# Late units of a state-space attention kernel: carry and scores in 32x32 tiles, heads paired q with 7-q, and one token per partition from the fifth unit on

## The chip, the cores and the metric

The kernel runs on one core of a Trainium2 chip. A core has TensorE (PE in the profile, with its weight loads as PEld), VectorE (DVE), ScalarE (ACT), GpSimd (POOL) and SyncE (SP), which issues most DMAs. Each engine works through its own list of instructions in order. The metric is the device time of one execution in microseconds (us).

## The reference

Two stages follow each other. The first is a chunked state-space attention with 4 batches, 8 heads, 768 tokens, head width 32 and state width 16:

```python
for c in range(nc):                       # chunks of the sequence
    cum = np.cumsum(log_a[chunk])
    L = np.exp(cum[:, None] - cum[None, :]) * causal
    y_intra = ((C @ B.T) * L) @ x         # inside the chunk
    y_inter = (C @ state) * np.exp(cum)   # from the state before
    state = np.exp(sum(la)) * state + B.T @ (x * np.exp(cum[-1] - cum))
```

The second is a feed-forward stage over all 3072 tokens (256 wide): `h = max(x @ w_in, 0)`, then `(h * h) @ w_out`, with 2048 hidden columns.

## The kernel before, in words

The tokens are cut into 12 units of 256 (three blocks of each of four batches); unit k is batch k mod 4, block k div 4. A unit is worked in two halves of 128 tokens, i = 0 and 1. The decay is folded into C and x beforehand (products with cumulated decay and with its reciprocal), so that the scores need only a causal mask.

For each unit, in this order:

- C, B and x are loaded by SyncE (`ph_load`, lines 121 to 136). Units below `LATE` (6) are loaded with two neighbouring tokens per partition in one DMA; later ones with one token per partition, one DMA for each half (line 129), and the x of units 8, 10 and 11 in two groups of heads besides.
- GpSimd scales C (`prep_c`, line 167), copies B to bf16 (`prep_b`, line 175) and scales x (`prep_x`, line 187). C and B land in `jt`, four heads side by side, heads q and q + 4 in one group of 32 columns.
- From unit 4 on a transposing DMA (`dma_tr`, line 196) makes `bct` of `jt`; before that TensorE does it.
- A *region* (`region`, line 421; from unit 4 on one per unit, named `rg4` to `rg12`) then does on TensorE, for the unit before (y) and the new one (u): the carry of y (the state times C, `ph_carry`, 128x128 matmuls against a block-diagonal spread state), the state update of u (`ph_u`), the products of y's masked scores with x (`ph_intra`), and the scores of u (`ph_mt`, lines 229 and 235). ScalarE copies y's result to `T` (`ph_t`) and u's update to `us`. VectorE masks u's scores (`ph_mask`, line 244), one bank of PSUM after another.
- VectorE advances the state (`ph_z`), and GpSimd spreads it over a block-diagonal tile `Sd` (`ph_sd`, line 371), which the next carry reads as weights.

Between the regions TensorE does the feed-forward stage of earlier units: `mm1` (line 450, four matmuls of 256 columns), ReLU on ScalarE (line 459), the square on VectorE (line 465), and `mm2` (line 481). From `rg4` on, PSUM banks 0 to 3 are the scores', 7 is `mm2`'s, and 4 to 6 go round between `mm1` and the regions, which take two.

The order of the work is written out by hand in the string `ORDER` (lines 48 to 69): each engine gets its instructions in the order in which the tokens stand there. A token is, for example, `ld4` (load unit 4), `pb5` (B of unit 5), `sa3` (spread state of unit 3, first half), `ml` (the mask of late units), `c1` (`mm1` and ReLU) or `C1` (`mm2`). On GpSimd the part around the first region reads `px4 pb5 pc5 sa3 px5 pq afC2 pc6 sa4`, and on SyncE `ld4`, C and B of unit 5, the transposes of unit 4 (`tr4`), x of unit 5, C of unit 6, `tr5`.

Of the kernel before, what the change touches and what calls it, by code (L numbers as in the profile page):

```python
# [30 lines left out]
def kernel(  # L31
# [38 lines left out]
    LATE = 6  # L70
# [23 lines left out]
    quad = const.tile([128, 4], FP32, name="quad")  # L94
# [11 lines left out]
    Pquad = const.tile([128, 24, 4], FP32, name="Pquad")  # L106
# [54 lines left out]
    def prep_c(k, eng, P=None):  # L161
        b, j = UNITS[k]
        p = P_sb if P is None else P
        st = 96 if P is None else 32
        col = (j * 32 if P is None else 0) + b * 8
        for g in range(2):
            eng.tensor_tensor(  # L167
                out=_fap(jt[k % 3], 128 + 144 * g, [[384, 2], [32, 4], [1, 16]]),
                in0=_fap(loaded[k]["C"], 128 * g, [[16, 2], [32, 4], [1, 16]]),
                in1=_fap(p, col + 4 * g, [[st, 2], [1, 4], [0, 16]]), op=ALU.mult)  # L170

    def prep_b(k, eng, gs=None):
        fn = eng.copy if eng is nc.scalar else eng.tensor_copy
        if gs is None:
            fn(out=_fap(jt[k % 3], 0, [[384, 2], [16, 2], [32, 4], [1, 16]]),  # L175
               in_=_fap(loaded[k]["B"], 0, [[16, 2], [128, 2], [32, 4], [1, 16]]))
            return
# [46 lines left out]
    def ph_mt(k):  # L224
        v = live[k]
        bct = v["bct"]
        for i in range(2 if k >= LATE else 0):
            for q in range(4):
                nc.tensor.matmul(pp[:, q, i * 256:i * 256 + 256], bct[32 * q:32 * q + 32, i, 0, :],  # L229
                                 _fap(bct[32 * q:32 * q + 32], i * 384 + 128, [[1, 256]]),  # L230
                                 start=True, stop=True, skip_group_check=True, tile_position=(32 * q, 0))
        for r in range(0 if k >= LATE else 2):
            for u in range(2):
                for q in range(4):
                    nc.tensor.matmul(  # L235
                        pp[64 * u:64 * u + 64, q, r * 256:r * 256 + 256],
                        bct[32 * q:32 * q + 32, r, 0, u * 64:u * 64 + 64],
                        _fap(bct[32 * q:32 * q + 32], 128 + u * 64, [[128, 2], [384, 2], [1, 64]]),
                        start=True, stop=True, skip_group_check=True,
                        tile_position=(32 * q, 64 * u))  # L240
        v["mts"] = big.tile([128, 4, 2, 2, 128], BF16, tag="mts", name=f"mts{k}")
# [21 lines left out]
    def ph_carry(k, h, begun):  # L263
        for i in range(2):
            S_i = live[k]["S"][i]
            if S_i is None:
                continue
            for g in range(2):
                mm(begun, h[i], range(4), pp[:, h[i], g * 128:(g + 1) * 128], S_i[:, g * 128:(g + 1) * 128],
                   _fap(live[k]["bct"], i * 384 + 128 + g * 128, [[1, 128]]) if k >= LATE else  # L270
                   _fap(live[k]["bct"], 128 + g * 128 + i * 64, [[384, 2], [1, 64]]), None)

    def ph_u(k, h, begun):
# [3 lines left out]
        if k >= LATE:  # L277
            for i in range(2 - last):
                for q in range(4):
                    mm(begun, h[i], [q], pp[32 * q:32 * q + 32, h[i], 256:320], jt[k % 3][:, i, 0, 32 * q:32 * q + 32],  # L280
                       _fap(v["xs"], i * 256 + q * 32, [[128, 2], [1, 32]]), (0, 32 * q))
            return
        for r in range(2):
            for i in range(2 - last):
                for q in range(4):
                    mm(begun, h[i], [q], pp[32 * q:32 * q + 32, h[i], 256:320],
                       jt[k % 3][64 * i:64 * i + 64, r, 0, 32 * q:32 * q + 32],
                       _fap(v["xs"][64 * i:64 * i + 64], r * 256 + q * 32, [[128, 2], [1, 32]]),
                       (64 * i, 32 * q))

    def ph_intra(k, h, begun, qs=range(4)):
        v = live[k]
        if k >= LATE:
            for i in range(2):
                for g in range(2):
                    for q in qs:
                        hd = 4 * g + q
                        mm(begun, h[i], [q], pp[32 * q:32 * q + 32, h[i], g * 128:(g + 1) * 128],
                           v["xs"][:, i, hd * 32:hd * 32 + 32], _fap(v["mts"], q * 512 + i * 256 + g * 128, [[1, 128]]),
                           (0, 32 * q))  # L300
            return
        for g in range(2):
            for r in range(2):
                for i in range(2):
                    for q in qs:
                        hd = 4 * g + q
                        mm(begun, h[i], [q], pp[32 * q:32 * q + 32, h[i], g * 128:(g + 1) * 128],
                           v["xs"][64 * i:64 * i + 64, r, hd * 32:hd * 32 + 32],
                           v["mts"][64 * i:64 * i + 64, q, r, g, :], (64 * i, 32 * q))

    def ph_t(k, h, engs=None):
        T[k] = tpool.tile([128, 2, 2, 2, 64], BF16, tag="T", name=f"T{k}")
        if k >= LATE:
            if h[1] == h[0] + 1:
                nc.scalar.copy(out=_fap(T[k], 0, [[128, 2], [256, 2], [1, 128]]),
                               in_=_fap(pp, h[0] * 512, [[512, 2], [128, 2], [1, 128]]))
                return
            for i in range(2):
                nc.scalar.copy(out=_fap(T[k], i * 128, [[256, 2], [1, 128]]), in_=_fap(pp, h[i] * 512, [[128, 2], [1, 128]]))
# [44 lines left out]
    def ph_sd(k, i):  # L364
        b, j = UNITS[k]
        v = live[k]
        if j == 2 and i == 1:
# [5 lines left out]
            in1=_fap(Pquad, 4 * total(i, b, j), [[0, 2], [1, 4], [0, 32]]), op=ALU.mult)  # L373
# [5 lines left out]
    def ph_sd_first(k):  # L379
# [6 lines left out]
            in1=_fap(Pquad, 4 * total(0, b, 0), [[0, 2], [1, 4], [0, 32]]), op=ALU.mult)  # L386
# [34 lines left out]
    def region(y=None, u=None, mt=None, late=False):  # L421

        h = sorted((bank(), bank()))
        begun = set()
        if y is not None:
            ph_carry(y, h, begun)
# [4 lines left out]
        if mt is not None:  # L431
# [10 lines left out]
    def mm1(blk, fp, c=None, h=None):  # L442
# [5 lines left out]
        for i in range(2):  # L448
            for g in range(2):
                nc.tensor.matmul(pp[:, h, i * 256:(i + 1) * 256] if c is None else  # L450
                                 _fap(pp, h * 512 + i * 256 + c * 64, [[128, 2], [1, 64]]),
                                 _fap(w, g * w.shape[2] + (o // 2) * 512 + 2 * (o % 2) + i, [[4, 128]]),
                                 T[blk][:, g].rearrange("p r u t -> p (r u t)") if c is None else T[blk][:, g, :, c],
                                 start=(g == 0), stop=(g == 1), skip_group_check=True)
# [18 lines left out]
    def mm2(blk, fp, rs=(0, 1), cols=None):  # L473
        h2 = h2s[(blk, fp)]
        gi, o = group_of(WOUT, fp)
        for i in range(2):
            for r in rs:
                first = fp == 0 and i == 0 and (r == 0 or blk == NU - 1)
                for c0, c1 in ((0, 256),) if cols is None and (blk < NU - 1 or r == 0) else cols or ((0, 128), (128, 256)):
                    dst = acc(blk, r) if c1 - c0 == 256 else pp[:, 1 + c0 // 128, 0:128]  # L480
                    nc.tensor.matmul(dst, h2[:, i, r * 128:(r + 1) * 128],  # L481
                                     w_out_b[gi][:, 2 * o + i, c0:c1], start=first, stop=(fp == 7 and i == 1),
                                     skip_group_check=True)
# [37 lines left out]
    with tc.manual_schedule():  # L521
# [47 lines left out]
        def quads():  # L569
            keep_if(quad, ones_f[:, 0:4], [[-32, 4]], 0, 1)  # L570
            keep_if(quad, quad, [[32, 4]], 31, -1)
# [11 lines left out]
        def picked():  # L583
            A.copy(out=_fap(spread, 0, [[32, 4], [16, 2], [1, 16]]), in_=_fap(heads, 0, [[1, 4], [4, 2], [0, 16]]))
# [14 lines left out]
        def first_quad():  # L599
            V.tensor_tensor(out=Pquad[:, 0:8], in0=_fap(pp, 4 * 512 + 64, [[1, 8], [0, 4]]),  # L600
                            in1=_fap(quad, 0, [[0, 8], [1, 4]]), op=ALU.mult)
# [27 lines left out]
        def second_quad():  # L629
            P.tensor_tensor(out=Pquad[:, 8:24], in0=_fap(Ptot, 8, [[1, 16], [0, 4]]),  # L630
                            in1=_fap(quad, 0, [[0, 16], [1, 4]]), op=ALU.mult)
# [110 lines left out]
        ups = {}  # L742

# [7 lines left out]
        def one(t):  # L751
# [5 lines left out]
            if len(name) == 1 and name.lower() in "abcdefghijkl" and len(f[0]) == 2:  # L757
# [7 lines left out]
                return  # L765
            if name[0] in "xryw" and len(name) == 2 and name[1] in "abcd":
                blk = "abcd".index(name[1])
                if name[0] in "xy":
                    ups[blk, k] = mm1(blk, k, None if name[0] == "x" else 0)
                    busy.add(ups[blk, k])  # L770
                elif name[0] == "w":
                    mm1(blk, k, 1, ups[blk, k])
                else:
                    busy.discard(ups[blk, k])
                    relu(blk, k, ups[blk, k])
# [97 lines left out]
```

## Time and profile before

| | |
|---|---|
| Runs | 113.6, 113.86 and 114.51 us, median 113.86 |
| Profiled execution | span 112.7 us from the first to the last instruction; no other time is given for it. The median lies 1.2 us above the span |
| TensorE | busy 106.8 us (95% of the span), 1449 matmuls |
| VectorE, ScalarE, GpSimd | busy 72%, 68%, 45% |
| DMA | 67281 packets, 63104 of them under 512 B; 13.44 MB |
| TensorE's granted clock | 1.000 |

The engines' busy shares overlap, since they work side by side. Matmuls are pipelined: in a list by time, a group of matmuls is given with the start of its first and the time to the end of its last one, so neighbouring groups overlap by the latency of one matmul. In the chain that ended last, each piece begins where the piece before ends. In square brackets stands how long an engine was idle before a group and what ended that.

### The profile page before, as it was taken

The page shows a single profiled execution, that of the slowest core. Times are in us where ns is not written, and L with a number is a line of the kernel's source. Part 1 is how long each engine was busy: PE and PEld are TensorE (multiplying, and loading weights), DVE is VectorE, ACT ScalarE, POOL GpSimd, SP SyncE. Part 2 cuts the span into 40 slices and gives each one's busy share as a digit, 9 for nine tenths or more (in the row PEclk, how much of TensorE's full clock was granted, in tenths as well). Part 3 has the DMA queues.
Part 4 walks back from the last instruction along what each step waited for, and adds up shares of the span by engine and source line. Part 5 has one row for each costly group of instructions (what it writes and reads, how often), then busy time and mean ns, then how long its engine had stood idle before and what let it go on. Part 6 is the DMA issues. An engine that isn't in the chain of part 4 may idle for free.

```text
span 112.7 us, 3678 instructions
## 1 busy us (share of the span) xinstructions
PE 106.8 (95%) x1449; PEld 92.3 (82%) x1450; DVE 80.7 (72%) x188; ACT 76.7 (68%) x158; POOL 50.2 (45%) x96
## 2 busy tenths in 40 slices
PE   7985799999999999999999999999999999999990
PEld 2433699897998989989979989889899899899980
DVE  1697867996793899969966989779588298355440
ACT  1554884986894785685687686777876867867840
POOL 7489961586476654394064792184440020000000
PEclk9999999999999999999999999999999999999999
DMA  1999999799979997979787878698950020020203
GB/s 32 194 191 184 197 210 212 127 178 192 154 137 82 125 268 79 118 192 66 100 160 87 162 152 92 134 145 102 185 126 0 6 96 0 25 68 6 93 0 93
DMA packets 67281, 13.44 MB, mean 119 GB/s; under 512 B 63104, under 2 KB 65984, under 8 KB 67264
## 3 DMA queue, kind: packets, MB, share of 16 engines
q1 hardware_dynamic: 64320, 10.88, 60.1%
q0 software_dynamic: 1664, 2.10, 11.1%
q10 hardware_dynamic: 1280, 0.23, 1.1%
q8 instruction: 11, 0.18, 0.6%
q14 instruction: 6, 0.05, 0.1%
HBM read 10.58 MB, written 3.15 MB: 122 GB/s over the span
## 4 chain that ended last, share of the span: by engine, by line
PE 88%; SPq 3%; DMA 3%; POOL 2%; ACT 1%; issue 1%; ACTq 0%; POOLq 0%
PE pp L450 38%; PE pp L481 38%; PE pp L260 7%; DMA C_nat<-in_C_dram 3%; PE pp L229 2%; PE pp L235 2%; SPq L642 1%; PE pp L205 1%; SPq L134 1%; POOL a_cl L604 1%; POOL w_in_b L148 1%; POOL jt L167 1%; ACT T L218 1%; ACT bct L218 0%; SPq L117 0%
## 5 line engine op out<-in xcount | busy, mean ns | idle before, releaser
L459 ACT ACTIVATE hb<-pp 128x512 bf16<-128x512 f32 x96 | 54.5, 601 | 21.7 <-PE pp L450 21.2
L450 PE MATMUL pp<-T,w_in_b 128*128 128x256 bf16 x384 | 53.4, 273 | 0.6 <-ACT T L218 0.6
L481 PE MATMUL pp<-w_out_b,h 128*128 128x256 bf16 (+1 forms) x400 | 53.8, 268 | 0.0
L465 DVE TENSOR_TENSOR h<-hb 128x512 bf16<-128x512 bf16 x96 | 41.9, 451 | 13.0 <-ACT hb L459 12.5
L450 PEld LDWEIGHTS <-w_in_b 128*128 128x128 bf16 x384 | 41.4, 114 | 2.6 <-issue 1.1
L481 PEld LDWEIGHTS <-h 128*128 128x128 bf16 x400 | 37.6, 98 | 4.5 <-issue 1.0
L244 DVE TENSOR_TENSOR mts<-pp,mask 128x512 bf16<-128x512 f32 x43 | 28.5, 677 | 1.4 <-PE pp L229 0.8
L187 POOL TENSOR_TENSOR xs<-x_nat,Pinv 128x256 bf16<-128x256 f32 (+1 forms) x19 | 13.8, 738 | 14.2 <-PE pp L260 6.9
L371 POOL TENSOR_TENSOR Sd<-z,Pquad 128x256 bf16<-128x256 f32 x16 | 10.6, 672 | 12.9 <-DVE z L355 6.7
L167 POOL TENSOR_TENSOR jt<-C_nat,P_sb 128x128 bf16<-128x128 f32 x22 | 9.4, 447 | 5.5 <-DMA C_nat<-in_C_dram 5.5
L355 DVE SCALAR_TENSOR_TENSOR z<-z,Ptot,us 128x64 f32<-128x64 f32 x8 | 3.6, 446 | 7.7 <-ACT us L339 5.2
L175 POOL CAST jt<-B_nat 128x256 bf16<-128x256 f32 x9 | 4.6, 512 | 5.7 <-DMA B_nat<-in_B_dram 5.7
L488 ACT COPY osb<-pp 128x512 f32<-128x512 f32 x11 | 6.4, 583 | 0.4 <-PE pp L481 0.4
L540 PE MATMUL pp<-const-bfloat16-1.0 128*128 128x512 bf16 (+1 forms) x15 | 5.9, 525 | 0.8 <-PEq L857 0.8
L260 PE MATMUL pp<-mts,xs 64*32 64x128 bf16 (+1 forms) x288 | 5.5, 219 | 0.0
L260 PE MATMUL pp<-bct,Sd 128*128 128x128 bf16 x40 | 4.2, 220 | 0.0
L260 PEld LDWEIGHTS <-xs 64*32 64x32 bf16 (+1 forms) x288 | 3.6, 93 | 0.4 <-issue 0.2
L540 PEld LDWEIGHTS <-const-bfloat16-1.0 128*128 128x128 bf16 x16 | 1.6, 121 | 2.3 <-issue 2.2
L205 PE MATMUL pp<-eye_b,jt 128*128 128x128 bf16 x24 | 2.4, 221 | 1.1 <-POOL jt L167 1.0
L205 PEld LDWEIGHTS <-jt 128*128 128x128 bf16 x24 | 1.7, 100 | 2.1 <-POOL jt L167 1.4
L220 DVE COPY bct<-pp 128x384 bf16<-128x384 bf16 (+1 forms) x7 | 2.3, 336 | 1.5 <-PE pp L205 0.8
L260 PEld LDWEIGHTS <-Sd 128*128 128x128 bf16 x40 | 3.0, 98 | 0.3
(76 smaller groups left out, 60.6 us busy)
## 6 DMA issues: line engine op xcount, KB each, us to landing
out_dram<-osb SPq DMA_DIRECT2D x11, 256.0 KB, 2.9
x_nat<-in_x_dram SPq DMA_DIRECT2D x6, 256.0 KB, 4.2
w_in_b<-in_moe_w_in_dram POOLq DMA_DIRECT2D x4, 256.0 KB, 7.0
w_out_b<-in_moe_w_out_dram POOLq DMA_DIRECT2D x4, 256.0 KB, 6.8
B_nat<-in_B_dram SPq DMA_DIRECT2D x6, 128.0 KB, 3.8
C_nat<-in_C_dram SPq DMA_DIRECT2D x12, 64.0 KB, 3.9
B_nat<-in_B_dram SPq DMA_DIRECT2D x12, 64.0 KB, 3.7
x_nat<-in_x_dram SPq DMA_DIRECT2D x6, 128.0 KB, 3.0
```

The costliest lines, as they stand in the source:

```text
L167: eng.tensor_tensor(out=_fap(jt[k % 3], 128 + 144 * g, [[384, 2], [32, 4], [1, 16]]), in0=_fap(loaded[k]["C"], 128 * g, [[16, 2], [32, 4], ...
L187: eng.tensor_tensor(out=_fap(xs, 256 * r, [[256, 2 // n], [32, 8], [1, 32]]), in0=_fap(loaded[k]["x"], 32 * r, [[32, 2 // n], [64, 8], [1, ...
L205: nc.tensor.transpose(pp[:, h, o:o + 64].bitcast(BF16), jt[k % 3][:, r, w, :], eye_b)
L244: nc.vector.tensor_tensor(out=live[k]["mts"][:, q].rearrange("p r g i -> p (r g i)"), in0=pp[:, q, :], in1=mask1 if k >= LATE else mask, o ...
L260: nc.tensor.matmul(dst, w, v, start=bool(need), stop=False, skip_group_check=True, **({} if pos is None else {"tile_position": pos}))
L371: nc.gpsimd.tensor_tensor(out=_fap(S_d, 0, [[128, 2], [32, 4], [1, 32]]), in0=_fap(z, 0, [[32, 2], [0, 4], [1, 32]]), in1=_fap(Pquad, 4 * ...
L450: nc.tensor.matmul(pp[:, h, i * 256:(i + 1) * 256] if c is None else _fap(pp, h * 512 + i * 256 + c * 64, [[128, 2], [1, 64]]), _fap(w, g ...
L459: nc.scalar.activation(out=hb.rearrange("p i t -> p (i t)"), in_=pp[:, h, :], func=AF.Relu)
L465: nc.vector.tensor_tensor(out=h2, in0=hb, in1=hb, op=ALU.mult)
L481: nc.tensor.matmul(dst, h2[:, i, r * 128:(r + 1) * 128], w_out_b[gi][:, 2 * o + i, c0:c1], start=first, stop=(fp == 7 and i == 1), skip_gr ...
L488: nc.scalar.copy(out=osb, in_=pp[:, 6 if blk == 1 else 7, :])
L540: nc.tensor.matmul(pp[:, h, 0:int(cols)], ones_b[:, 0:128], ones_b[:, 0:int(cols)] if dep is None else dep, start=True, stop=True, skip_gr ...
```

## The change

- `LATE` goes from 6 to 4: units 4 and 5 are also loaded with one token per partition, by two DMAs for each of C, B and x, and are worked in the late form. Their output is written in pieces half as long. The decay factors are made for all units after the first four in one form (the interleaved matmuls in line 507 fall away). The mask of late units (`ml`) is made earlier.
- Heads are paired q with 7 - q in place of q with q + 4, in `jt`, `bct`, the spread state and the masks. `Pquad` holds a second, mirrored pattern for that, so the second half of the spread state is block-antidiagonal.
- In the regions of units 5 to 11 (`fine`), the carry is 16 matmuls of 32x32 instead of four of 128x128, and the scores are 32 of 32x32 instead of eight of 32x128. The scores stand directly behind the carry, ahead of the state update and the products.
- In late units a bank holds four heads of both halves, instead of all eight heads of one half.
- B's copy is always two instructions. The x of units 8, 10 and 11 is no longer loaded in two groups of heads. Some unused code goes.

```diff
-        ldB6:s ldx6:s qc4 qc0 A6 px5 pq A7 wm c2 B6 c7 C0 ms3:v mk3 qc6 mk3 qc7 afC2 pc6 B7 C3 C6 C4 qc1 bk rg4 C1 qc2
+        ldB6:s ldx6:s qc4 qc0 A6 px5 pq ml A7 wm c2 B6 c7 C0 ms3:v mk3 qc6 mk3 qc7 afC2 pc6 B7 C3 C6 C4 qc1 bk rg4 C1 qc2
-        mk5 d5 qd4 D2 pc7 pb7 d6 qd5 d7 qd6 D3 zb2 e0 qd7 mk5 e1 qe0 sb2 D4 mk5 D5 tr7 ld8 e2 qe1 D6 e3 qe2 ml px7 rg6
+        mk5 d5 qd4 D2 pc7 pb7 d6 qd5 d7 qd6 D3 zb2 e0 qd7 mk5 e1 qe0 sb2 D4 mk5 D5 tr7 ld8 e2 qe1 D6 e3 qe2 px7 rg6
...
-    LATE = 6
+    LATE = 4
...
-    Pquad = const.tile([128, 24, 4], FP32, name="Pquad")
+    Pquad = const.tile([128, 24, 8], FP32, name="Pquad")
...
-    def prep_b(k, eng, gs=None):
+    def prep_b(k, eng, gs=(0, 1)):
...
         for g in gs:
             fn(out=_fap(jt[k % 3], 16 * g, [[384, 2], [32, 4], [1, 16]]),
-               in_=_fap(loaded[k]["B"], 128 * g, [[16, 2], [32, 4], [1, 16]]))
+               in_=_fap(loaded[k]["B"], 224 * g, [[16, 2], [32 - 64 * g, 4], [1, 16]]))
...
+    def ph_mt(k, fine=False):
+        m = 32 if fine else 128 if k >= LATE else 64
+        for r in range(2):
+            for c in range(0, 128, m):
                 for q in range(4):
+                    p = slice(32 * q, 32 * q + 32)
                     nc.tensor.matmul(
+                        pp[c:c + m, q, r * 256:r * 256 + 256], bct[p, r, 0, c:c + m],
+                        _fap(bct[p], r * 384 + 128, [[1, 256]]) if k >= LATE else
+                        _fap(bct[p], 128 + c // 64 * 64, [[128, 2], [384, 2], [1, 64]]),
+                        start=True, stop=True, skip_group_check=True, tile_position=(32 * q, c))
...
+    def ph_carry(k, h, begun, fine=False):
...
+            for e in range(2):
+                if fine:
+                    for q in range(4):
+                        c = 3 - q if e else q
+                        mm(begun, h[e], [c], pp[32 * c:32 * c + 32, h[e], i * 128:(i + 1) * 128],
+                           S_i[32 * q:32 * q + 32, e * 128 + 32 * c:e * 128 + 32 * c + 32],
+                           _fap(bct[32 * q:32 * q + 32], i * 384 + 128 + e * 128, [[1, 128]]), (32 * q, 32 * c))
+                    continue
...
     def ph_t(k, h, engs=None):
...
-                nc.scalar.copy(out=_fap(T[k], 0, [[128, 2], [256, 2], [1, 128]]),
-                               in_=_fap(pp, h[0] * 512, [[512, 2], [128, 2], [1, 128]]))
+                nc.scalar.copy(out=_fap(T[k], 0, [[256, 2], [1, 256]]), in_=_fap(pp, h[0] * 512, [[512, 2], [1, 256]]))
...
+        fine = mt is not None and y >= LATE
         if y is not None:
-            ph_carry(y, h, begun)
+            ph_carry(y, h, begun, fine)
+        if fine:
+            ph_mt(mt, fine)
         if u is not None:
             ph_u(u, h, begun)
         if y is not None:
             ph_intra(y, h, begun)
-        if mt is not None:
+        if mt is not None and not fine:
             ph_mt(mt)
...
         def load_all(k):
             for what in "CBx":
-                for hs in ((0, 4), (4, 8)) if what == "x" and k in (8, 10, 11) else ((0, 8),):
-                    ph_load(k, what, hs=hs)
+                ph_load(k, what)
```

More of the change, by code (lines that the diff above doesn't have):

```diff
@@ L93 @@
     warm = const.tile([128, 2], BF16, name="warm")
-    quad = const.tile([128, 4], FP32, name="quad")
+    quad = const.tile([128, 8], FP32, name="quad")
     pick = const.tile([128, 16], FP32, name="pick")
@@ L583, in picked @@
         def picked():
-            A.copy(out=_fap(spread, 0, [[32, 4], [16, 2], [1, 16]]), in_=_fap(heads, 0, [[1, 4], [4, 2], [0, 16]]))
+            for g in range(2):
+                A.copy(out=_fap(spread, 16 * g, [[32, 4], [1, 16]]), in_=_fap(heads, 7 * g, [[1 - 2 * g, 4], [0, 16]]))
             A.activation(out=pick_p[0], in_=pick[0:64, 0:8], func=AF.Copy, scale=cp[0][:, 127:128])
```

120 lines of the change are left out of this document (45 added, 75 removed).

## The prediction

> **What bounds the kernel.** I read the page's shares first, then the chain that ended last, then the stretches that the change touches. From the page:
>
> ```profile
> span 112.7 us, 3678 instructions
> PE 106.8 (95%) x1449; PEld 92.3 (82%) x1450; DVE 80.7 (72%) x188; ACT 76.7 (68%) x158; POOL 50.2 (45%) x96
> DMA  1999999799979997979787878698950020020203
> PE 88%; SPq 3%; DMA 3%; POOL 2%; ACT 1%; issue 1%; ACTq 0%; POOLq 0%
> ```
>
> TensorE is busy for 95% of the span and carries 88% of the chain, so an instruction taken from it is time gained, and a wait put on it is time lost. The third line says what may put one there: the DMA engines are nearly full (nines, with a seven between) from 3 to about 42 us. The chain in order of time, where it turns to TensorE for good, and at the regions, the bursts of small matmuls at which units 4, 5, 6 and 7 enter:
>
> ```profile
> 14.70 2.69 PE pp L450 x24
> ...
> 35.68 0.61 PE pp L260 x50
> 36.30 0.35 PE pp L235 x16
> ...
> 40.69 0.73 PE pp L260 x52
> 41.42 0.35 PE pp L235 x16
> ...
> 47.99 0.74 PE pp L260 x44
> 48.73 0.33 PE pp L229 x8
> ...
> 56.61 0.62 PE pp L260 x28
> 57.23 0.33 PE pp L229 x8
> ```
>
> From the first of these rows on the chain is TensorE alone, piece against piece; 24 matmuls of 256 columns in 2.69 us are 0.11 each. The regions of units 4 to 7 cost 0.96, 1.08, 1.07 and 0.95 us. Nothing waits there today; the question is what the change takes off these pieces, and whether it makes one of them wait.
>
> **Part 1: units 4 and 5 in the late layout.** The region of unit 7 has the late form throughout, that of unit 6 early carry and products with late scores. So the region of unit 5 goes from 1.08 to 0.95 (-0.13), that of unit 6 from 1.07 to 0.95 (-0.12). The region of unit 4 becomes today's unit 6 region with two carry matmuls fewer: 1.07 less 2 x 0.056 (the pitch is worked out below) is 0.96, so 0. Together -0.25 us. The decay factors lose their interleaved matmuls in line 507:
>
> ```profile
> 13.78 0.42 PE L507 MATMUL pp<-eye_f,cp 128*64 128x16 f32 x8
> 13.87 0.42 DVE L383 TENSOR_TENSOR Sd<-pp,Pquad 128x256 bf16<-128x256 f32 x1 [0.47 <-PE pp L260]
> 14.04 0.37 PE L511 MATMUL pp<-eye_f,cp 128*64 128x96 f32 x4
> 14.42 0.29 PE L260 MATMUL pp<-bct,Sd 128*128 128x128 bf16 x2
> ```
>
> That removes 0.26 us (13.78 to 14.04) and widens the four after it by a third, perhaps 0.06. But the next carry reads the state that VectorE finishes at 14.29, so it can move from 14.42 only to about 14.35: -0.07, and -0.20 if that state were early too. Masks, copies of T and state products keep their sizes.
>
> **Part 2: carry and scores in 32x32 tiles.** A late region today, by start times on TensorE:
>
> ```profile
> 72.52 0.39 PE L260 MATMUL pp<-bct,Sd 128*128 128x128 bf16 x4
> 72.83 0.21 PE L260 MATMUL pp<-xs,jt 128*32 128x64 bf16 x4
> 72.87 0.40 PE L260 MATMUL pp<-mts,xs 128*32 128x128 bf16 x16
> 73.20 0.40 PE L229 MATMUL pp<-bct 32*128 32x256 bf16 x8
> 73.53 0.62 PE L450 MATMUL pp<-T,w_in_b 128*128 128x256 bf16 x4
> ```
>
> A group's time ends with its last matmul, whose own latency is about 0.22 us for 128 columns. So the four carries start over 0.39 - 0.22 = 0.17 us, a pitch of 0.056. Sixteen products in four tiles start over 0.18, again four rounds of 0.056: the four column tiles run side by side. Between different tile shapes about 0.09 us pass empty (the last carry's slot ends at 72.75, the next starts at 72.83). The region takes 73.53 - 72.52 = 1.01 us with three such changes of shape. The new one also has three (into 32x32 ahead of the carry, to 128x32, to 128x128). The carry falls from four slots of 0.056 to two, if eight tiles run side by side; the scores keep two rounds of 256 columns, now 16 matmuls a round.
>
> What speaks against a gain is the number of instructions: 16 + 32 matmuls, each with its weights, in one run, where 4 + 8 stood. Today's nearest row is a run of 48 in the unit 4 region:
>
> ```profile
> 35.72 0.25 PE L260 MATMUL pp<-xs,jt 64*32 64x64 bf16 x16
> 35.79 0.51 PE L260 MATMUL pp<-mts,xs 64*32 64x128 bf16 x32
> ```
>
> The first 16 start within 35.79 - 35.72 = 0.07 us, so 0.004 each; all 48 need 35.79 + 0.51 - 0.22 - 35.72 = 0.36 us. Eight tiles side by side would need only four rounds of 0.056 after the first 16, about 0.25. The last ones come 0.10 late: the instructions run short. With 0.36 us to the last start the new region is 0.09 + 0.36 + 0.11 + 0.09 + 0.28 (products and state updates as today) + 0.09 = 1.02, no gain. If the supply keeps up, the last score starts after 2 x 0.056 + 0.107 + 0.05 = 0.27, and the region takes 0.93. Seven regions (units 5 to 11): between -0.6 and +0.1 us. I take 0, by the run of 48.
>
> On the Trainium skill: its page "TensorE: Matmul & The Clock Gate" (Part 3, the mechanism) gives the engine a 64-deep window and packed tiles about 4 ns apart. The trace agrees with the 4 ns, and 64 instructions are 32 matmuls with weights, beyond which the row above falls behind. By the page's span model alone the region would be near the 0.93.
>
> The scores now stand ahead of the products, so the copy of T loses its cover:
>
> ```profile
> 73.32 0.58 ACT L315 CAST T<-pp 128x512 bf16<-128x512 f32 x1
> ```
>
> It is done at 73.90; the matmuls that need the freed bank start two groups of four after the region, at 73.53 + 8 x 0.11 = 74.41. The copy comes some 0.33 later relative to the region's end (73.53 - 73.20, one score block), which leaves 0.18 for the small copy behind it. I count 0; where that is short, up to 0.1 a region, 0.5 in all.
>
> **Part 3: the loads, which decide.** Units 4 and 5 now need six load issues each instead of three, of pieces half as long, in the full stretch of the DMA line. SyncE's queue, for the C and B of units 4, 5, 9 and 10:
>
> ```profile
> 22.15 0.58 SPq L134 DMA_DIRECT2D C_nat<-in_C_dram  x1
> 22.83 0.79 SPq L134 DMA_DIRECT2D B_nat<-in_B_dram  x1
> ...
> 24.73 0.76 SPq L134 DMA_DIRECT2D C_nat<-in_C_dram  x1
> 25.59 1.18 SPq L134 DMA_DIRECT2D B_nat<-in_B_dram  x1
> ```
>
> ```profile
> 55.90 1.18 SPq L129 DMA_DIRECT2D C_nat<-in_C_dram  x2
> 57.12 3.01 SPq L129 DMA_DIRECT2D B_nat<-in_B_dram  x2
> ...
> 65.36 1.40 SPq L129 DMA_DIRECT2D C_nat<-in_C_dram  x2
> 66.81 1.38 SPq L129 DMA_DIRECT2D B_nat<-in_B_dram  x2
> ```
>
> Today's pairs take 1.47 and 2.04 us, mean 1.76; the same data in late form 4.23 and 2.83. So each pair costs +1.07 by the calmer late row and +2.47 by the worse. With both pairs and 0.2 for the split x of unit 4, unit 5's B arrives 2.3 us later; at least 1.6 (2.83 against 2.04, twice); at most 3.7 (one pair at the worse price). Who waits for it is GpSimd:
>
> ```profile
> 31.70 0.65 POOL L175 CAST jt<-B_nat 128x256 bf16<-128x256 f32 x1 [2.29 <-DMA B_nat<-in_B_dram]
> 32.31 0.97 POOL L167 TENSOR_TENSOR jt<-C_nat,P_sb 128x128 bf16<-128x128 f32 x2
> 33.25 0.61 POOL L371 TENSOR_TENSOR Sd<-us,Pquad 128x256 bf16<-128x256 f32 x1
> ```
>
> ```profile
> 35.41 0.21 PEld L260 LDWEIGHTS <-Sd 128*128 128x128 bf16 x2
> ```
>
> GpSimd takes its list in order, and unit 3's spread state (line 371) stands behind unit 5's B and C. It is done at 33.86, and TensorE loads it as the carry's weights at 35.41. That is 1.55 us of slack. With B 2.3 later it is done at 36.16, and TensorE, 0.07 early by then, waits 36.16 + 0.05 - 35.34 = 0.9 us, with 0.05 for the hand-over. Bounds: 0.2 and 2.3. The B cast in two halves is counted at 0: what it adds lies in the same wait and is a part of 0.65.
>
> ```profile
> 37.81 0.61 POOL L371 TENSOR_TENSOR Sd<-z,Pquad 128x256 bf16<-128x256 f32 x1
> ...
> 48.69 0.90 POOL L544 TENSOR_SCALAR_AFFINE_SELECT mask<-const-bfloat16-1.0 128x512 bf16<-128x512 bf16 x1
> ```
>
> The later mask (second row) moves ahead of unit 6's C product and so ahead of unit 4's spread state (first row). That one is done at 38.42, some 2 us before the carry of unit 5's region (40.69 on the chain), and the 0.9 that TensorE has lost by then covers the mask; what the loads add is the second rival's. Later units have the x of units 8, 10 and 11 in two issues instead of four, which pays the queue back. I count 0 for them.
>
> **Sum.** -0.25 - 0.07 + 0 + 0.9 = +0.6 us on a span of 112.7. The median of the runs is 113.86, 1.2 above the span, and I leave that part alone: 114.4 us. About 1% (1.1 us) is what a measurement of this kernel can tell from no change.
>
> **Rivals.**
> - *The late load is hidden.* If unit 5's B comes less than 1.4 us later, the carry does not wait. For it: the queue sits in transposes for part of this stretch, and the added issues could fall there. Against it: the nines. Then -0.3, and with a supply that keeps up -0.9: 112.9 to 113.5. This one ends on the faster side.
> - *The delay travels on.* SyncE's list has no long rest, so the 2 to 4 us may reach unit 5's transpose, unit 4's spread state behind the mask, or unit 8's transpose, which is queued behind the B row at 57.12 (and is needed earlier now, with the scores first). A second wait of about 1 us gives 115.4 to 116.
> - *The 32x32 carries do not run side by side.* Four row tiles write one bank, in different partitions, which no row of today shows. One after another, 16 slots of 0.056 take 0.9 in place of 0.11: +0.8 in each of seven regions, so 114.4 + 5.5 = 119.9. For: today's kernel never does it. Against: the tiles share no partition of the bank. The Trainium skill's page "TensorEngine Tiling (Array Packing)", Gotcha 1, says that different row tiles cannot access the same bank at once; by that rule this rival holds.
> - *The late form saves nothing in units 4 and 5*, and the wait stays: 114.7.
>
> **Chances.** Forecast with the last rival 0.55 (own range 113.7 to 115.3), hidden load 0.23, delay that travels 0.17, carries one by one 0.05. A range of 112.9 to 116.0 leaves out the last, and a tenth more at the ends. Faster by over 1% (below 112.7) needs the hidden load, full supply and the 0.20 of part 1: 0.05. Slower by over 1% (above 115.0): 0.17 + 0.05 + a fifth of 0.55, 0.33. Within 1%: 0.62.
>
> **What would show it.** A wait of TensorE for GpSimd's Sd of line 371 near 35.5 us, and GpSimd's wait for B ahead of it at 34 in place of 31.7. The regions of units 5 and 6 near 1.0. The start of the last score 0.36 after the first carry (0.27: the supply keeps up; over 0.9: the carries go one by one). I am wrong if SyncE issues unit 5's B no later than 27 us, or if another engine than GpSimd holds up the region of unit 4.

## The result, and the profile after

| | before | after |
|---|---|---|
| Median of the runs beside each other | 114.02 us (4 runs) | 117.4 us (4 runs, 117.26 to 118.64) |
| Ratio, 95% interval | | 1.032 [1.026, 1.038] |
| Profiled execution: span | 112.7 us | 115.4 us (time 117.43 us) |

The change makes the kernel 3.2% slower; 114.4 us was forecast, and 116.0 was the end of the range. (Medians here are of all executions; ratios leave out the disturbed ones.)

The page of the changed kernel, first the lines that answer to those shown of before:

```profile
span 115.4 us, 4050 instructions
PE 107.2 (93%) x1630; PEld 91.6 (79%) x1630; DVE 81.9 (71%) x188; ACT 77.1 (67%) x161; POOL 52.3 (45%) x106
DMA  2999999789998979999997895896993020020202
DMA packets 73682, 13.46 MB, mean 117 GB/s; under 512 B 69248, under 2 KB 72640, under 8 KB 73664
PE 68%; DMA 8%; SPq 7%; ACT 5%; POOL 3%; issue 3%; DVE 2%; POOLq 0%; ACTq 0%
```

TensorE works as long as before (107.2 us, 106.8 before) in a span 2.7 us longer. The chain has left it: 68% instead of 88%, and 15% lie with DMA and SyncE's issues. Nearly the same bytes (13.46 MB, 13.44 before) travel in 73682 packets instead of 67281. What TensorE waits for (engine, line, releaser; us in total, times, longest):

```profile
PE pp L252 <- POOL Sd L371: 2.7, 2, 1.9
...
PE pp L454 <- ACT T L214: 0.6, 1, 0.6
```

The first row is as large as the growth of the span: two waits for a spread state (`Sd`, GpSimd, line 371), 2.7 us; before had none. The list of TensorE by time shows where they stand, and the chain of waits what lies behind the first:

```profile
37.18 0.29 PE L252 MATMUL pp<-bct,Sd 128*128 128x128 bf16 x2 [1.89 <-POOL Sd L371]
...
42.31 0.25 PE L252 MATMUL pp<-bct,Sd 32*32 32x128 bf16 x8
43.38 0.25 PE L252 MATMUL pp<-bct,Sd 32*32 32x128 bf16 x8 [0.82 <-POOL Sd L371]
```

```profile
31.96 2.85 DMA B_nat<-in_B_dram
35.83 0.72 POOL jt L167 x2
36.55 0.58 POOL Sd L371
37.18 0.81 PE pp L252 x42
```

One wait is at unit 4's region, one at unit 5's. Behind the first stands a load of B (unit 5's), then GpSimd's product for C, then the spread state. GpSimd's list by time:

```profile
35.30 0.52 POOL L175 CAST jt<-B_nat 128x128 bf16<-128x128 f32 x2 [2.70 <-DMA B_nat<-in_B_dram]
35.79 0.76 POOL L167 TENSOR_TENSOR jt<-C_nat,P_sb 128x128 bf16<-128x128 f32 x2
36.51 0.61 POOL L371 TENSOR_TENSOR Sd<-us,Pquad 128x256 bf16<-128x256 f32 x1
...
38.94 0.73 POOL L545 TENSOR_SCALAR_AFFINE_SELECT mask<-const-bfloat16-1.0 128x512 bf16<-128x512 bf16 x1
...
41.53 1.01 POOL L167 TENSOR_TENSOR jt<-C_nat,P_sb 128x128 bf16<-128x128 f32 x2 [1.73 <-PE pp L454]
42.50 0.82 POOL L371 TENSOR_TENSOR Sd<-z,Pquad 128x256 bf16<-128x256 f32 x1
```

Unit 5's B is taken at 35.30 instead of 31.70, 3.6 us later, and unit 3's spread state behind it is done at 37.12 instead of 33.86, 3.3 us later. The second wait has the same form: unit 4's spread state (42.50) stands behind unit 6's C (41.53), with GpSimd idle for 1.73 us ahead of it. Before, that C was taken at 37.10:

```profile
37.10 0.76 POOL L167 TENSOR_TENSOR jt<-C_nat,P_sb 128x128 bf16<-128x128 f32 x2 [0.35 <-DMA C_nat<-in_C_dram]
```

The profile puts the 1.73 us of the changed kernel down to TensorE; its DMA records have the second half of unit 6's C landing at 41.30, and an experiment below moves it out of the way. The mask (38.94) is done 1.9 us before.

SyncE's issues, after and before (start, duration, count):

```profile
19.50 3.32 SPq L134 DMA_DIRECT2D x_nat<-in_x_dram  x1
22.86 1.35 SPq L129 DMA_DIRECT2D C_nat<-in_C_dram  x2
24.31 2.12 SPq L129 DMA_DIRECT2D B_nat<-in_B_dram  x2
26.48 3.19 SPq L129 DMA_DIRECT2D x_nat<-in_x_dram  x2
29.76 1.22 SPq L129 DMA_DIRECT2D C_nat<-in_C_dram  x2
31.08 1.46 SPq L129 DMA_DIRECT2D B_nat<-in_B_dram  x2
```

```profile
19.94 2.16 SPq L134 DMA_DIRECT2D x_nat<-in_x_dram  x1
...
23.66 0.98 SPq L134 DMA_DIRECT2D x_nat<-in_x_dram  x1
```

Unit 4's x costs SyncE 3.19 us instead of 0.98, its C and B 3.57 (22.86 to 26.43) instead of 1.47, unit 5's C and B 2.78 instead of 2.04. Unit 5's B is issued 5.5 us later (31.08, 25.59 before).

Last a late region in the new form, unit 9's, which waits for nothing:

```profile
74.73 0.60 PE L482 MATMUL pp<-w_out_b,h 128*128 128x256 bf16 x4
75.26 0.25 PE L252 MATMUL pp<-bct,Sd 32*32 32x128 bf16 x8
...
75.35 0.58 PE L228 MATMUL pp<-bct 32*32 32x256 bf16 x27
...
76.23 0.63 PE L454 MATMUL pp<-T,w_in_b 128*128 128x256 bf16 x4
```

A 32x32 matmul with 128 columns lasts 0.21 to 0.22 us alone; eight of them end 0.25 after the first starts, so they start within 0.04. They run side by side. The last score starts at 75.35 + 0.58 - 0.28 = 75.65, 0.39 after the first carry. For what a region costs I take, here and below, the time from the start of the last feed-forward matmul ahead of it (0.11 apart in a group) to the first behind it: here 76.23 - 75.06 = 1.17 us. The same region of before costs 73.53 - 72.41 = 1.12, by these rows:

```profile
72.08 0.60 PE L481 MATMUL pp<-w_out_b,h 128*128 128x256 bf16 x4
...
73.53 0.62 PE L450 MATMUL pp<-T,w_in_b 128*128 128x256 bf16 x4
```

### The profile page after: what moved, and what is told of

It is laid out like the page before. It is cut to its first block, busy times and chain, and to the rows that moved or that the text cites. A ratio compares the mean times of both kernels' runs of the same rounds, so it can differ in the third digit from the quotient of the medians.

```text
span 115.4 us, 4050 instructions
## 1 busy us (share of the span) xinstructions
PE 107.2 (93%) x1630; PEld 91.6 (79%) x1630; DVE 81.9 (71%) x188; ACT 77.1 (67%) x161; POOL 52.3 (45%) x106
## 2 busy tenths in 40 slices
DMA packets 73682, 13.46 MB, mean 117 GB/s; under 512 B 69248, under 2 KB 72640, under 8 KB 73664
## 4 chain that ended last, share of the span: by engine, by line
PE 68%; DMA 8%; SPq 7%; ACT 5%; POOL 3%; issue 3%; DVE 2%; POOLq 0%; ACTq 0%
PE pp L454 29%; PE pp L482 29%; PE pp L252 6%; SPq L134 5%; DMA B_nat<-in_B_dram 5%; ACT hb L461 4%; PE pp L228 3%; DMA C_nat<-in_C_dram 3%; SPq L645 1%; DVE h L467 1%; POOL Sd L371 1%; POOL jt L167 1%; POOL xs L183 1%; PE pp L201 1%; ACT T L214 1%
## 5 line engine op out<-in xcount | busy, mean ns | idle before, releaser
L467 DVE TENSOR_TENSOR h<-hb 128x512 bf16<-128x512 bf16 x96 | 44.0, 478 | 11.3 <-ACT hb L461 10.9
L183 POOL TENSOR_TENSOR xs<-x_nat,Pinv 128x256 bf16<-128x256 f32 (+1 forms) x19 | 13.3, 706 | 11.1 <-DMA x_nat<-in_x_dram 5.7
L167 POOL TENSOR_TENSOR jt<-C_nat,P_sb 128x128 bf16<-128x128 f32 x22 | 10.2, 486 | 10.4 <-DMA C_nat<-in_C_dram 8.7
L355 DVE SCALAR_TENSOR_TENSOR z<-z,Ptot,us 128x64 f32<-128x64 f32 x8 | 2.8, 354 | 12.0 <-ACT us L339 6.9
L175 POOL CAST jt<-B_nat 128x128 bf16<-128x128 f32 x19 | 6.2, 353 | 7.3 <-DMA B_nat<-in_B_dram 7.3
L252 PE MATMUL pp<-bct,Sd 32*32 32x128 bf16 (+1 forms) x124 | 3.8, 220 | 2.8 <-POOL Sd L371 2.7
L228 PE MATMUL pp<-bct 32*32 32x256 bf16 (+2 forms) x296 | 6.3, 275 | 0.1
L252 PEld LDWEIGHTS <-Sd 32*32 32x32 bf16 (+1 forms) x124 | 1.8, 88 | 4.9 <-POOL Sd L371 3.1
L316 ACT CAST T<-pp 128x512 bf16<-128x512 f32 x6 | 3.5, 585 | 2.8 <-PE pp L252 2.8
L228 PEld LDWEIGHTS <-bct 32*32 32x32 bf16 (+2 forms) x296 | 3.3, 91 | 1.6 <-DVE bct L216 0.9
```

The costliest lines, as they stand in the source:

```text
L167: eng.tensor_tensor(out=_fap(jt[k % 3], 128 + 144 * g, [[384, 2], [32, 4], [1, 16]]), in0=_fap(loaded[k]["C"], 224 * g, [[16, 2], [32 - 64 ...
L183: eng.tensor_tensor(out=_fap(xs, 256 * r, [[256, 2 // n], [32, 8], [1, 32]]), in0=_fap(loaded[k]["x"], 32 * r, [[32, 2 // n], [64, 8], [1, ...
L228: nc.tensor.matmul(pp[c:c + m, q, r * 256:r * 256 + 256], bct[p, r, 0, c:c + m], _fap(bct[p], r * 384 + 128, [[1, 256]]) if k >= LATE else ...
L252: nc.tensor.matmul(dst, w, v, start=bool(need), stop=False, skip_group_check=True, **({} if pos is None else {"tile_position": pos}))
L467: nc.vector.tensor_tensor(out=h2, in0=hb, in1=hb, op=ALU.mult)
```

## The experiments

The main theory is the forecast's: the loads of units 4 and 5, in pieces half as long, hold GpSimd's list, and through it two carries. Rivals: the 32x32 form itself, the mask and the split copies of B on GpSimd, the number of issues rather than the pieces.

**Loads and form, each undone.** `late6` sets back the loads and layout of units 4 and 5; `nofine` sets back the shapes and the place of the scores.

```diff
-    LATE = 4
+    LATE = 6
```
```diff
-        fine = mt is not None and y >= LATE
+        fine = False
```

> The changed kernel with LATE at 6 again: pairing of heads, 32x32 carry and scores (now in the regions of units 7 to 11) and order of scores stay; the loads of units 4 and 5 are as before the change. Theory, the late loads of units 4 and 5 make GpSimd and so TensorE wait: both waits go, five regions cost 0.04 us more each, 114.2 us, between 113.7 and 114.6. Rival, the 32x32 form itself costs the time: about 116.5. Rival, the split B copy and the mask make GpSimd late: 116 or more.

> The changed kernel with the carry at 128x128 and the scores at 32x128 in all late regions, scores behind the products; LATE stays 4. Theory, the loads decide: both waits on GpSimd stay, seven regions are 0.04 us shorter, 117.1 us, between 116.7 and 117.4. Rival, the 32x32 form costs the time: about 114.5.

`late6` has a median of 115.65 us (four executions, 114.19 to 116.6; 113.7 to 114.6 was forecast); its waits for `Sd` are gone, and the regions of units 4 and 5 cost 1.18 and 1.29 us as before. `nofine` has 117.34 us, ratio 1.024 [1.014, 1.034]: without the 32x32 form most of the loss stays. So the loads carry most of it, and the form something. That both waits stay in `nofine`, as forecast, isn't shown: in its profiled execution, of 118.01 us, TensorE had lost time before (waits of 1.8 and 0.8 us, the last of them at 29.05) and came to unit 4's region only at 38.12, when the spread state, done at 37.91, was there.

**Before with shorter pieces, or with more issues.** Both edits are made to the kernel before, for units 4 and 5: `cut` loads one token of each pair with each of two DMAs (half the length, twice the pieces), `two` loads four heads with each of two DMAs (the same pieces).

```diff
+        if k in (4, 5):
+            for r in range(2):                       # cut
+                (eng or nc.sync).dma_start(out=_fap(t[what], r * w, [[2 * w, 8], [1, w]]),
+                    in_=_dap(src, (b * NH * S + j * 256) * w + r * w, [[2 * w, 128], [S * w, 8], [1, w]]))
+            return
```
```diff
+        if k in (4, 5):
+            for h0 in (0, 4):                        # two
+                (eng or nc.sync).dma_start(out=t[what][:, h0:h0 + 4],
+                    in_=_dap(src, ((b * NH + h0) * S + j * 256) * w, [[2 * w, 128], [S * w, 4], [1, 2 * w]]))
+            return
```

> The kernel before the change with one edit: C, B and x of units 4 and 5 are loaded by two DMAs each, one per token of a pair, so in pieces half as long, into the same places. Theory, the pieces of the loads delay unit 5's B, and GpSimd's list holds unit 3's spread state behind it: TensorE waits 1.5 to 2.2 us at unit 4's region, and up to 0.8 at unit 5's, 116.3 us, between 115.5 and 117. Rival, the split copies, the mask and the wider products on GpSimd made it late: 114.0 to 114.4.

> The kernel before the change with one edit: C, B and x of units 4 and 5 are loaded by two DMAs each, four heads and four heads, so twice the issues on SyncE but pieces of the same length and number. If the number of pieces (DMA work) makes the delay: 114.0 to 114.5, no wait on GpSimd at unit 4. If the issues on SyncE make it: as with the pieces cut, 115.5 to 117.

`cut` (73521 packets): 116.91 us, ratio 1.023 [1.015, 1.030]. `two` (67377 packets): 114.58 us, ratio 1.002 [0.998, 1.007]. The waits of TensorE in `cut`:

```profile
PE pp L266 <- POOL Sd L377: 1.4, 1, 1.4
...
PE pp L235 <- DMA bct<-jt: 0.7, 1, 0.7
```

Twice the issues cost nothing that can be told (one wait of 0.21 us for `Sd`, at unit 5's region); twice the pieces, with nothing else of the change, bring the wait at unit 4's region and 2.3%. In the DMA records of before a piece of 128 bytes occupies an engine for 13.1 ns and one of 64 for 11.8, on average: half the bytes take nearly the same time. The second row is a transpose that comes late (unit 8's), the third place of the forecast's *delay travels on*.

**Longer pieces.** `longpieces` is the changed kernel with C, B and x of units 4 and 5 loaded from 1024 tokens on end, in pieces of 512 and 1024 bytes. These aren't the tokens of the reference; the bytes and the work are the same.

```diff
+        if k in (4, 5):
+            for i in range(2):
+                (eng or nc.sync).dma_start(out=_fap(t[what], i * 8 * w, [[1, 8 * w]]),
+                    in_=_dap(src, (b * NH * S + j * 256) * w + i * 1024 * w, [[8 * w, 128], [1, 8 * w]]))
+            return
```

> The changed kernel, but C, B and x of units 4 and 5 come in pieces of 512 and 1024 B (128 long rows in place of 1024 pieces, as many bytes, two DMAs each as in the changed kernel); the rows are other tokens and heads than the reference asks for, so what is computed of these two units is left out of the comparison with the reference. Theory, the short pieces are the whole cost: no wait at the regions of units 4 and 5, and what is left of the change is the 32x32 form (7 x 0.04) against the late form's 0.25 in units 4 to 6: 114.0 us, between 113.4 and 114.5. Rival, split B copies, mask and pairing on GpSimd have a part: over 115.

The ratio to before falls from 1.032 to 1.008 [1.003, 1.012]. No wait for `Sd` is left, and the span of its profile is 112.3 us, 3.1 below that of the changed kernel. So the waits come of the pieces; the late form of units 4 and 5, the split copies of B, the pairing and the mask are all still in this kernel. The forecast of 114.0 fits the profiled execution (114.1); the median of the ten is 115.88, over the end of its range, and the 0.8% that is left is of the size that the 32x32 form costs in the table below.

**What stands behind the late loads on GpSimd.** `sa3` puts unit 3's spread state ahead of unit 5's B, `pc6` puts unit 4's ahead of unit 6's C, `both` does both.

```diff
-  px4 tr4 ldx5:s pb5 pc5 sa3 c1
+  px4 sa3 tr4 ldx5:s pb5 pc5 c1
```
```diff
-  afC2 pc6 B7 ... za4 sa4 pb6
+  afC2 B7 ... za4 sa4 pc6 pb6
```

> The changed kernel, and on GpSimd's list unit 3's spread state ahead of unit 5's B and C instead of behind them. Theory A, the loads set the time and the list only decides where TensorE meets them: the 2 us wait at unit 4's region goes, and the wait at unit 5's region grows from 0.8 to nearly 3, since unit 4's spread state still stands behind unit 6's C, which lands at its own time: 117.2 us, between 116.6 and 117.5. Theory B, the waits add up, and each goes with its place in the list: 115.4.

> The changed kernel, and on GpSimd's list unit 4's spread state ahead of unit 6's C instead of behind it. Both theories: the 2 us wait at unit 4's region stays, the 0.8 us at unit 5's goes, or shrinks to what unit 5's transpose then takes (it landed at 42.4, the region begins at 42.3): 116.6 us, between 116.3 and 117.0. If the mask ahead of that spread state made the wait, it stays: 117.4.

> The changed kernel with both moves on GpSimd's list. Theory A, the loads set the time: no wait at unit 4's region, then one of about 2 us for unit 5's transpose (due at 42.4, the region begins at 40.3): 116.4 us, between 115.8 and 116.9. Theory B, the list sets it: no wait, 114.5.

`sa3`: 117.39 us, ratio 1.027 [1.022, 1.032]. `pc6`: 116.53 us, 1.018 [1.011, 1.025]. `both`: 117.39 us, 1.019 [1.014, 1.024]. The profiled executions took 118.62, 117.62 and 120.59 us, each the longest of its four, so their waits are read here and not their spans. In `pc6` unit 5's region costs 1.20 and waits for nothing, with the mask still ahead of the spread state: it was unit 6's C. (The wait at unit 4's region stays, at 2.00 us, and the clock granted from 38 to 41 us is 0.54.) In `sa3` unit 4's region costs 1.17 and waits for nothing, but the time comes back one region later, by the waits of TensorE and the list by time in `sa3`:

```profile
PE pp L228 <- DVE mts L236: 0.8, 2, 0.7
PE pp L252 <- POOL Sd L371: 0.6, 1, 0.6
```

```profile
40.16 1.04 PE L482 MATMUL pp<-w_out_b,h 128*128 128x256 bf16 x8
...
41.97 0.25 PE L252 MATMUL pp<-bct,Sd 32*32 32x128 bf16 x8 [0.60 <-POOL Sd L371]
...
42.47 0.26 PE L228 MATMUL pp<-bct 32*32 32x256 bf16 x1 [0.16 <-DVE mts L236]
43.40 0.43 PE L228 MATMUL pp<-bct 32*32 32x256 bf16 x29 [0.67 <-DVE mts L236]
...
44.16 1.61 PE L482 MATMUL pp<-w_out_b,h 128*128 128x256 bf16 x8
```

The scores of unit 5 stand ahead of the products now, and need the banks whose scores of unit 4 VectorE is still masking. Theory A's time came, but only 0.6 us of it is the wait for `Sd` that it named. The last row shows a second thing: eight matmuls of 256 columns take 1.61 us instead of 1.04. By stretches (TensorE busy first, granted clock and DMA share near the end):

```profile
41.00:44.00 3.00, 1.58 (x71) 0.75 (x72) 3.00 (x8) 1.07 (x2) 1.46 (x4) 1.00 0.93 132
44.00:48.00 4.00, 4.00 (x38) 2.88 (x25) 3.45 (x8) 1.35 (x3) 2.57 (x4) 0.57 1.14 190
```

TensorE was busy for 1.58 of 3 us, and in the four after them it is granted 0.57 of its clock. In `both` unit 5's region costs 4.32 us, with waits for the masks of 1.3 us and the clock at 0.57 from 43 to 47 us; the wait for unit 5's transpose that theory A had there is missing, and so is the gain of theory B.

**The mask.** Unit 4's masks need the late mask, which stands on GpSimd behind x of unit 5. `both_mask` is `both` with that mask made before x of unit 2.

```diff
-  iv:16:32 px2 ... px5 pq ml A7
+  iv:16:32 ml px2 ... px5 pq A7
```

> The changed kernel with both spread states moved ahead, as in `both`, and the mask of late units made on GpSimd before x of unit 2 is scaled, near 21 us, instead of behind x of unit 5, near 40 us. Theory (in `both` the masks of unit 4 waited for the late mask, and the scores of unit 5, which now stand ahead of the products, waited for the banks that those masks had yet to read): no wait of TensorE for VectorE's mts, no stretch at half the granted clock behind it, unit 5's region 1.2 to 1.8 us instead of 4.3, time 115.0 to 115.8. Rival (the masks of unit 4 are late for another reason, such as VectorE's own list): the wait for mts stays, region over 3 us, time near 117.4.

> A second look at the same kernel, for its waits: those of the theory above have to be the same in both profiles if they are the kernel's and not the execution's.

The second label is the same kernel again, in spite of its name. The waits for masks are gone in both profiles, unit 5's region costs 1.20 us, and the clock stays full: on the masks the theory holds, on the time it doesn't. The profiled executions took 115.48 and 116.46 us, the median of four is 116.94 (115.0 to 115.8 was forecast), and the ratio is 1.018 [1.008, 1.029]. What is late next is a transpose in each, at unit 4's scores in the first profile:

```profile
37.29 0.40 PE L228 MATMUL pp<-bct 32*128 32x256 bf16 x8 [1.55 <-DMA bct<-jt]
...
40.69 1.04 PE L482 MATMUL pp<-w_out_b,h 128*128 128x256 bf16 x8
...
42.65 1.05 PE L482 MATMUL pp<-w_out_b,h 128*128 128x256 bf16 x8
```

and at unit 8's in the second:

```profile
66.47 0.44 PE L228 MATMUL pp<-bct 32*32 32x256 bf16 x32 [1.50 <-DMA bct<-jt]
```

The reorderings win back less than half of the 3.2% (1.018 at best), since each wait taken away uncovers the next late transfer.

**What the 32x32 form costs, with the loads as before.** Four kernels with `LATE` = 6: as `late6` (`late6_again` and `late6_third`, the same kernel twice more); the scores behind the products again (`late6_last`); the scores first in the old shapes (`late6_first`); and neither (`late6_nofine` and `late6_nofine_again`, the same kernel).

```diff
-        if fine:
-            ph_mt(mt, fine)
...
-        if mt is not None and not fine:
-            ph_mt(mt)
+        if mt is not None:                           # late6_last
+            ph_mt(mt, fine)
```
```diff
-            ph_carry(y, h, begun, fine)
+            ph_carry(y, h, begun)                    # late6_first
...
-            ph_mt(mt, fine)
+            ph_mt(mt)
```

> The changed kernel with LATE = 6, so that units 4 and 5 are loaded and worked as before, and the heads' pairing and the 32x32 form of the regions of units 7 to 11 stay. Theory (the loads of units 4 and 5 are the loss; the 32x32 form costs 0.03 to 0.04 us in each of five regions, 0.2 in all): 114.2 to 114.4, a ratio of 1.001 to 1.004. Rival (a further loss sits in what is left of the change): over 1.007.

> As late6_again, with carry and scores of all late units in the old shapes and the scores last. Regions of units 7 to 11 back at 1.12 to 1.15 us; theory: 0.2 us below late6_again, a ratio of 0.999 to 1.002. Rival (32x32 costs nothing beside what a region hides): the same time as late6_again.

> LATE = 6, 32x32 tiles and scores first. Theory A (the form costs what its regions show, 0.19 us, and the rest of late6_again's loss was the chip): ratio 1.001 to 1.004. Theory B (scores that come 0.4 us earlier meet a late transpose or bank in many executions, though not in the profiled ones): 1.008 to 1.02.

> As late6_third, with the 32x32 scores behind the products, where they stood before. Theory A: within 0.003 of late6_third. Theory B: 1.000 to 1.003, well below late6_third.

> As late6_third, with the scores first but carry and scores in the old shapes. Theory A: 0.999 to 1.003. Theory B: as late6_third, 1.008 to 1.02.

> Old shapes, scores last. Both theories: 0.998 to 1.003, as late6_nofine.

| ratio to before | units 4 and 5 loaded as before | one token per partition |
|---|---|---|
| old shapes, scores last | 1.001 [0.997, 1.005]; 1.003 [1.001, 1.006] | 1.024 [1.014, 1.034] |
| old shapes, scores first | 1.002 [0.998, 1.005] | not run |
| 32x32, scores first | 1.016 [1.007, 1.025]; 1.009 [1.004, 1.013] | 1.032 [1.026, 1.038] (the change) |
| 32x32, scores last | 1.021 [1.017, 1.026] | not run |

In the old shapes the place of the scores costs nothing that can be told; in 32x32 tiles the scores last came out no better. The 32x32 shapes cost 0.9 to 2.1% in the timed executions. So neither theory on record holds, A by the size, B by the place. The regions don't show it: those of units 7 to 11 cost 5.84 us together in `late6` and 5.65 in `late6_nofine`, 0.2 us. Two more profiles of `late6_last` were taken to find the rest:

> If the 32x32 form costs time in its regions, the regions of units 7 to 11 grow beyond 1.20 us in some execution. If the time goes in the first 35 us, before any 32x32 matmul has run, the region of unit 4 begins later than the 35.2 us of late6_nofine_again, and the distance from there to the end of the span stays within 0.5 us of its 77.5.

> As late6_last_look: a further execution of the same kernel, read for the start of unit 4's region and for the distance from there to the end.

The first took 114.43 us, the second 116.44. Their lists of TensorE, unit 4's carry and the last matmuls, first of the one and then of the other:

```profile
34.87 0.28 PE L252 MATMUL pp<-bct,Sd 128*128 128x128 bf16 x2
...
106.93 2.38 PE L480 MATMUL pp<-w_out_b,h 128*128 128x256 bf16 x30
```

```profile
36.38 0.28 PE L252 MATMUL pp<-bct,Sd 128*128 128x128 bf16 x2
...
108.45 2.37 PE L480 MATMUL pp<-w_out_b,h 128*128 128x256 bf16 x30
```

Their last two issues on SyncE, for the output, of the one and of the other:

```profile
109.07 0.82 SPq L819 DMA_DIRECT2D out_dram<-osl  x2
```

```profile
110.58 1.61 SPq L819 DMA_DIRECT2D out_dram<-osl  x2
```

From the carry to the last group pass 72.06 and 72.07 us, and all regions agree to 0.01. The slower execution lost 1.51 us before its unit 4, and so before its first 32x32 matmul, and 0.6 behind the last (from its end to the end of the span 3.88 instead of 3.29). The distance from unit 4's region to the end, 77.7 and 78.3 us, is 0.3 and 0.9 above the 77.4 of `late6_nofine_again`; the second is past the 0.5 that the expectation gave. The other kept profiles agree. In the six with the form at `LATE` = 6, unit 4's carry starts between 34.87 and 36.68 us, and from there to the end pass 77.7 or 78.3 us; wherever it is 78.3 (`late6`, `late6_third` and the second one here), the two issues take 1.61 to 1.65 us, else 0.82. In the three without it, the carry starts between 35.02 and 35.30, and 77.4 to 77.5 us are left. In `late6_last` a further part of the time lies outside the span (116.23 us, span 113.6).

So the 32x32 work itself costs the 0.2 us in each profiled execution. Why kernels with the form spend more before unit 4 and behind the last matmul, in some executions and not in others, stays open. They have 4041 instructions instead of 3681; that this does it is not shown.

## Why the prediction was wrong

- **The place was right.** TensorE waits for `Sd` of line 371 at unit 4's region, GpSimd for unit 5's B ahead of it, and SyncE issues that B well after 27 us.
- **The step that failed is the size of the load delay**, the term of 2.3 us in part 3. Measured are 3.6 at GpSimd, near the bound of 3.7 given there, and 3.3 at the spread state, and so 1.9 us of wait instead of 0.9. Of the 5.8 us by which the issue of that B ends later (32.54, 26.77 before), the two pairs of C and B make 2.8, where the forecast took 2.1; the split x of unit 4, counted at 0.2, made 2.2; and 0.7 stood ahead in the queue (unit 3's x). GpSimd sees 3.6 of it, as B's second half landed 2.85 us after its issue began (row at 31.96 of the chain above), where B took 5.96 before, by the DMA records.
- **The second step that failed** counted unit 4's spread state at nothing, as the time that TensorE has lost would cover it. It covered the mask, but not unit 6's C, which came 4.4 us later on GpSimd: 0.8 us more. This is the rival *the delay travels on* with its price of about 1 us. I gave it 0.17, though the queue that makes the first wait makes the second: the two were one case.
- **The late form's gain came about as forecast.** In `nofine`, which has the late form without the 32x32 tiles, unit 6's region costs 51.51 - 50.36 = 1.15 us, against 48.99 - 47.72 = 1.27 of before: -0.12, as forecast. In the changed kernel it costs 1.19; the difference is what the 32x32 form costs in other regions too. Unit 5's region costs 1.22 in `nofine` against 1.29 (-0.13 was forecast), with a carry of 0.44 instead of 0.39 us there, as its spread state is done only at 43.34. The rows of before and of `nofine`:

```profile
47.39 0.60 PE L450 MATMUL pp<-T,w_in_b 128*128 128x256 bf16 x4
...
48.99 0.63 PE L450 MATMUL pp<-T,w_in_b 128*128 128x256 bf16 x4
```

```profile
50.03 0.60 PE L454 MATMUL pp<-T,w_in_b 128*128 128x256 bf16 x4
...
51.51 0.62 PE L454 MATMUL pp<-T,w_in_b 128*128 128x256 bf16 x4
```

- **The 32x32 term** was counted at 0 by the run of 48: last start 0.36 after the first, measured 0.39, and 0.03 to 0.05 us a region, 0.2 in five regions and 0.3 in seven: the argument holds, and the size lies above the -0.6 to +0.1 us given. In the timed executions the form costs 0.9% or more; the rest of that isn't in the regions, and no step of the prediction named it. The Trainium skill's page "TensorE: Matmul & The Clock Gate" (Part 3, the mechanism) has packed tiles start about 4 ns apart. The case that the prediction ties to it, a supply that keeps up, gave 0.27 for the last start; the trace says 0.39, so the run of 48 was the better guide.
- **Carries one by one** (119.9) fell: eight start within 0.04 us. The Trainium skill's "TensorEngine Tiling (Array Packing)", Gotcha 1, has different row tiles unable to use a bank at once; here four of them write one bank, each in partitions of its own, and nothing queues.
- **The copy of T** lost its cover at no price: TensorE's only wait for T in the list above (0.6, line 214) is an early one, and `late6_first` is at 1.002.
- **The gain in the decay factors** (-0.07) can't be told from what the first 35 us vary by themselves.
- **The sum.** The spans differ by 2.7 us, where 0.6 was forecast. The waits make 1.8 of the 2.1 between them (1.9 + 0.8 instead of 0.9), the 32x32 regions 0.3. The medians differ by 3.4, and part of that lies in the base, a term that the forecast left alone: it took the median to lie 1.2 above the span, but in later executions time and span mostly lie 1.7 apart. By that, before's span of 112.7 goes with an execution of about 114.4, near the slowest of the three and not the median.

## What to carry to other kernels

- Price a split load by its pieces, not by its bytes or issues: here a piece of 64 bytes held a DMA engine for 11.8 ns and one of 128 for 13.1, so the same data in halves took 1.8 times the engine time; the DMA line was full, and everything queued behind them on SyncE moved with it.
- Where engines take their lists in order, a late transfer delays all that stands behind its first reader; ask of each what TensorE takes from it. Moving one item ahead only shows the next late transfer, so mend the transfer.

## What the runs showed of the hardware that was not expected

- The granted clock can fall without one long idle time: in `sa3` TensorE was busy for 1.58 of 3.00 us, its longest idle time 0.67, and was then granted 0.57 over 4 us. The clock's changes within one trace lie whole multiples of 3.41 us apart. In `pc6` the wait of 2.00 us lies in one such stretch (33.92 to 37.33 us, TensorE busy for 1.41), and the clock is halved for the next; in the changed kernel the wait of 1.89 us is split between two (2.50 and 2.44 busy), and the clock stays full. No sharp bound shows: 1.86 busy of 3.41 brought no fall in `both_mask`, 2.20 came ahead of one in `both`. The Trainium skill's page "TensorE: Matmul & The Clock Gate", Part 1, has a free-running window of about 3.4 us, and ties the fall to an idle one. The traces agree on the length; no stretch here was idle throughout.
- The switch into 32x32 tiles leaves 75.26 - 75.06 = 0.20 us between two starts, where 128x128 matmuls of 256 columns stand 0.11 apart.
- The same program can take 2 us longer by what passes in its first 35 us and behind its last matmul, at the full clock (114.43 and 116.44 us).
